# A new order, new buffers and new engines for every task of an RWKV and token-mixer kernel

## The chip, the cores and the metric

The kernel runs on one core of a Trainium2 chip. Its time is the device time of one execution in microseconds; the median of three runs of the kernel before is 160.68 us (159.12 to 160.82).

The engines are named as the profile names them: PE is TensorE's matmul stream and PEld its weight loads, DVE is VectorE, ACT is ScalarE, POOL is GpSimd, SP is SyncE, which here only issues DMAs. DMAs are issued from SP (loads of k, r and v, transposes, stores), from POOL (loads that also change the type: v of the first batch and all weights) and from ACT (small ones).

## The reference, cut to what matters

The inputs are r, k, v of 4 batches x 8 heads x 768 steps x 48 elements, and a decay w and a bonus u for each head and element. All are float32.

```python
for t in range(S):
    cur = einsum('bhd,bhe->bhde', u * k[t], v[t])
    y[t] = einsum('bhd,bhde->bhe', r[t], state + cur)
    state = w * state + einsum('bhd,bhe->bhde', k[t], v[t])
x = y as (4, 768, 384)
h = max(x.transpose @ w_tok1, 0) @ w_tok2        # 768 -> 256 -> 768, over the steps
u = x + h.transpose
out = u + max(u @ w_ch1, 0) @ w_ch2              # 384 -> 1536 -> 384
```

## The kernel before, in words

A batch is cut into six chunks of 128 steps. For a chunk, r and k are scaled by powers of the decay (tiles `kr`, one product on DVE or POOL for each), turned on PE or by a DMA, and multiplied with each other on PE to a 128 x 128 table of scores for each head (`at_ps`). DVE masks it (`AT`), PE multiplies it with v and adds what the state carries over (`y_ps`), and k and v are multiplied into the state (`kv_ps`). The term of u is a sum over r, u and k (`adg`), multiplied with v (`yd`, `ydb`). The result, `x_b`, goes to the mixer of the batch: two matmuls over the steps (`h_ps` from `wtok`, `hT_ps` or `hx_ps`), twelve blocks of "up" products for each half of the batch (`z_ps` from `wch`), each with a ReLU on ACT or DVE (`zr`), and the "down" products (`h_ps` from `zr`), with a sum on DVE or ACT and a store.

The first batch is done in pairs of chunks (`pair_unit`): three pairs of 256 steps, each with one load of k, one of r and one of v into the three parts of a tile `zr` (`room`, `homes`). Here the first pair's tile is `zr_121`, the second's `zr_104`, the third's `zr_163`; after the change they are `zr_104`, `zr_103` and `zr_105`. `load_v` issues the loads of v from POOL. In the second batch r is loaded in pairs too (`win`). The attention of a batch is interleaved with the mixer of the batch before it.

Every piece of work is a task with a number. `Plan.run` emits the tasks in the order of the table `ORDER`, and the engines keep that order. `BUFS` says which buffer each tile takes, and `ENGINES` which of two engines does each task that either may do. So the queues hold no surprise: what an engine does next is what stands next in its order, and it waits there until its inputs have come. `mul_k`, `mul_r` and `scaled` are the products into `kr`; `turned` and `turn_r` are the transposes on PE (`tk_ps`, `tr_ps`); `load_weights` issues the seven loads of weights, `w0` (w_tok1) to `w6` (last part of w_ch2).

`keep_warm` makes `NWARM` = 20 products of a tile of zeros (`warm`, 128 x 512) into a `kv_ps` bank. They are the zero products; nothing reads what they give.

All instructions of the kernel's body have the line 274 in the profile (276 after the change), so that they are told apart by their tiles.

The loop that emits the tasks, and the load of v:

```python
for n in self.order:
    emit, deps = self.tasks[n]
    assert done.issuperset(deps), n
    self.now = n
    emit()
    done.add(n)
...
t = homes[b, c][:, 2].bitcast(bf16)[:, 0:H // 2].rearrange("p h (z j d) -> p (h z) j d", z=2, j=2)
what = v[b, :, ds(c * T, 2 * T), :].rearrange("h (p j) d -> p h (j d)", j=2)
asked[b, c, 2] = pool.dma_start(t.rearrange("p h j d -> p h (j d)"), what)
```

Of the kernel before, what the change touches and what calls it, by code (L numbers as in the profile page):

```python
# [78 lines left out]
    0, 0, 0, 0,  # L79
    ],  # L80
    'adg': [
    0, 1, 2, 3, 4, 1, 0, 2, 3, 4, 1, 0, 2, 1, 3, 4, 0, 1,
    ],
    'adg2': [
    0, 1, 0,
# [1143 lines left out]
```

## Time and profile before

| | |
|---|---|
| median of the runs | 160.68 us (159.12 to 160.82) |
| span of the profiled execution | 157.6 us |
| time of that execution beyond its span | not shown by the page |
| PE busy | 152.7 us, 97% |
| DVE busy | 114.5 us, 73% |
| POOL busy | 78.0 us, 49% |
| ACT busy | 68.3 us, 43% |
| moved by DMA | 26.60 MB, mean 169 GB/s |

Times within the execution count from the start of its span. The chain of waits is followed back from the last instruction to what released it, and so on; it is shown in order of time. In a timeline, a bracket behind a row gives the idle time of the engine ahead of it and what ended it. A row may hold several instructions of one kind (x8); its length is then that of all. Instructions on PE overlap by their pipeline, so that the distance from one start to the next is what a piece costs.

### The profile page before, as it was taken

To read this page: it belongs to the slowest core of one execution; us is meant where nothing else is said; L and a number is where in the kernel's file an instruction comes from. 1 tells how busy PE (TensorE), PEld (TensorE's weight loads), DVE (VectorE), ACT (ScalarE), POOL (GpSimd) and SP (SyncE) were. 2 spreads that over 40 slices of the span, in tenths; PEclk is the share of its full clock that TensorE was granted. 3 is DMA by queue.
4 is the path that set the end of the run, shared out by engine and by line. 5 is a ranking of instruction groups with operands and counts; after the bars stand their busy time and mean duration, and the time that the engine had idled before them with its cause. 6 is when DMAs were issued, how large, how long until landed. Compare 5 with 4: busy or idle time off the path is not lost.

```text
span 157.6 us, 3939 instructions
## 1 busy us (share of the span) xinstructions
PE 152.7 (97%) x1564; PEld 102.4 (65%) x1564; DVE 114.5 (73%) x237; ACT 68.3 (43%) x154; POOL 78.0 (49%) x103
## 2 busy tenths in 40 slices
PE   6999999999999999999999999999999999999992
PEld 1375866777776676677767666677667666666661
DVE  5479894698697976889899978948998392544332
ACT  3876765749666363132851141179324102550100
POOL 7798689000996848945784445966814000000000
DMA  4999999999999999999999999999891066010423
GB/s 121 266 246 188 165 195 215 191 242 157 185 198 222 198 186 194 224 226 224 161 187 211 177 217 199 175 222 218 100 251 31 24 154 175 0 50 4 150 75 125
DMA packets 88005, 26.60 MB, mean 169 GB/s; under 512 B 82738, under 2 KB 87092, under 8 KB 87988
## 3 DMA queue, kind: packets, MB, share of 16 engines
q1 hardware_dynamic: 82512, 22.52, 73.8%
q0 software_dynamic: 5280, 3.74, 15.7%
q8 instruction: 12, 0.20, 0.5%
q10 hardware_dynamic: 196, 0.11, 0.2%
q14 instruction: 5, 0.04, 0.1%
HBM read 20.46 MB, written 4.72 MB: 160 GB/s over the span
## 4 chain that ended last, share of the span: by engine, by line
PE 95%; DVE 1%; ACT 1%; issue 1%; DVEq 0%; ACTq 0%
PE h_ps L274 36%; PE z_ps L274 30%; PE kv_ps L274 7%; PE y_ps L274 6%; PE at_ps L274 4%; PE hT_ps L274 4%; PE tr_ps L274 2%; PE hx_ps L274 2%; PE tk_ps L274 1%; PE w_ps L274 1%; PE trk L274 1%; PE ad_ps L274 1%; PE u_ps L274 1%; DVE pr L274 0%; ACT rkb L274 0%
## 5 line engine op out<-in xcount | busy, mean ns | idle before, releaser
L274 PE MATMUL h_ps<-wch,zr 128*128 128x384 bf16 (+1 forms) x300 | 52.7, 320 | 0.0
L274 PE MATMUL z_ps<-uT,wch 128*128 128x384 bf16 x288 | 50.5, 326 | 0.0
L274 ACT ACTIVATE zr<-z_ps 128x384 bf16<-128x384 f32 x63 | 28.5, 495 | 40.3 <-PE z_ps L274 40.2
L274 PEld LDWEIGHTS <-wch 128*128 128x128 bf16 x288 | 31.5, 114 | 12.5
L274 PEld LDWEIGHTS <-zr 128*128 128x128 bf16 x300 | 27.8, 98 | 16.1
L274 DVE TENSOR_SCALAR zr<-z_ps 128x384 bf16<-128x384 f32 x33 | 17.5, 553 | 9.8 <-PE z_ps L274 8.4
L274 DVE TENSOR_TENSOR AT<-at_ps,mask 128x512 bf16<-128x512 f32 x36 | 23.1, 684 | 1.4 <-PE at_ps L274 1.3
L274 POOL TENSOR_TENSOR kr<-kt,wnat 128x384 bf16<-128x384 f32 x13 | 13.0, 1004 | 9.9 <-DMA kt<-in_k_dram 4.3
L274 DVE TENSOR_TENSOR osb<-u_sb,h_ps 128x384 f32<-128x384 bf16 (+1 forms) x19 | 10.1, 531 | 9.6 <-PE h_ps L274 7.7
L274 POOL TENSOR_TENSOR yd<-vb,adg 128x384 f32<-128x384 bf16 x15 | 12.7, 849 | 7.3 <-ACT vb L274 5.8
L274 PEld LDWEIGHTS <-kr 128*128 128x128 bf16 (+1 forms) x196 | 12.4, 101 | 4.6 <-issue 1.8
L274 ACT CAST S<-kv_ps 48x192 bf16<-48x192 f32 (+1 forms) x26 | 8.8, 338 | 10.1 <-PE kv_ps L274 8.3
L274 POOL TENSOR_TENSOR ku<-kt,u_bc 128x384 f32<-128x384 f32 x10 | 9.9, 1001 | 4.4 <-DVE rku L274 2.8
L274 POOL TENSOR_TENSOR rku<-ku,rt 128x384 f32<-128x384 f32 x10 | 10.2, 1021 | 2.6 <-DVE ku L274 2.1
L274 PEld LDWEIGHTS <-wtok 128*128 128x128 bf16 x84 | 8.0, 98 | 5.1
L274 DVE TENSOR_TENSOR x_b<-y_ps,yd 128x384 bf16<-128x384 f32 x18 | 9.7, 553 | 2.2 <-PE y_ps L274 2.1
L274 DVE TENSOR_TENSOR u_sb<-x_b,hT_ps 128x384 bf16<-128x384 bf16 x18 | 8.9, 550 | 3.3 <-PE hT_ps L274 3.2
L274 POOL TENSOR_TENSOR kr<-rt,wp 128x384 bf16<-128x384 f32 x9 | 9.1, 1010 | 2.3 <-ACT wp L274 2.3
L274 ACT CAST vb<-vt 128x384 bf16<-128x384 f32 x14 | 7.1, 516 | 5.9 <-DMA vt<-in_v_dram 5.9
L274 PE MATMUL kv_ps<-warm 128*128 128x512 bf16 x20 | 8.0, 505 | 1.5 <-DVE warm L274 1.5
L274 PE MATMUL h_ps<-x_b,wtok 128*128 128x384 bf16 x48 | 8.6, 326 | 0.0
L274 DVE TENSOR_REDUCE adg<-rku 128x8 f32<-128x384 f32 x12 | 6.6, 546 | 1.7 <-POOL rku L274 1.7
(108 smaller groups left out, 189.3 us busy)
## 6 DMA issues: line engine op xcount, KB each, us to landing
out_dram<-osb SPq DMA_DIRECT2D x23, 192.0 KB, 2.3
kt<-in_k_dram SPq DMA_DIRECT2D x18, 192.0 KB, 5.6
vt<-in_v_dram SPq DMA_DIRECT2D x18, 192.0 KB, 3.9
rt<-in_r_dram SPq DMA_DIRECT2D x12, 192.0 KB, 3.8
wch<-in_moe_w_ch_dram POOLq DMA_DIRECT2D x4, 384.0 KB, 7.4
zr<-in_k_dram SPq DMA_DIRECT2D x3, 384.0 KB, 4.7
zr<-in_r_dram SPq DMA_DIRECT2D x3, 384.0 KB, 6.0
win<-in_r_dram SPq DMA_DIRECT2D x3, 384.0 KB
```

Of the source, the lines that this page charges most:

```text
L274: return lambda *args, **kw: tc.keep_in_program_order(f(*args, **kw))
```

## The change: what it does

All of `ORDER`, `BUFS` and `ENGINES` are new tables. The tasks and their number are the same, and so is the code that makes them. A line of each:

```diff
 ORDER = [
-    9, 57, 26, 3, 46, 0, 886, 884, 880, 1, 17, 8, 4, 6, 27, 24, 56, 59, 18, 19, 20, 10, 60, 2, 62, 878, 887,
...
+    3, 57, 56, 58, 60, 9, 49, 0, 45, 59, 8, 26, 881, 2, 10, 22, 62, 1, 880, 23, 42, 877, 63, 27, 4, 7,
...
     'kp': [
-    0, 1, 2, 3, 4, 5, 1, 3, 0, 5, 2, 1, 4, 3, 2, 0, 1, 5, 3, 4, 0, 2, 5, 0, 3, 1, 4,
+    0, 1, 2, 3, 4, 5, 1, 3, 0, 5, 1, 2, 4, 0, 3, 5, 2, 4, 0, 1, 3, 5, 2, 0, 4, 3, 1,
...
 ENGINES = [
-    0, 0, 0, 0, 1, 1, 0, 0, 1, 0, 1, 1, 0, 1, 0, 0, 0, 0, 1, 0, 1, 1, 0, 1, 0, 0, 0, 1, 0, 0, 0, 1, 0, 0, 0,
...
+    0, 0, 0, 0, 1, 0, 0, 1, 1, 1, 1, 1, 0, 0, 0, 1, 0, 0, 0, 0, 1, 1, 0, 0, 1, 0, 0, 0, 0, 0, 0, 0, 0,
```

Where the instructions then stand shows what moves. The first place is the start of POOL's order. Before, from its nineteenth row:

```order
L274 TENSOR_TENSOR kr0_67<-zr_121,u_sb_166 128x8x48
L274 MEMSET mask_80 128x128
L274 AFFINE_SELECT mask_80<-mask_80 128x128
L274 DMA zr_121<-in_v_dram 128x8x96
L274 DMA zr_104<-in_v_dram 128x8x96
L274 DMA zr_163<-in_v_dram 128x8x96
L274 TENSOR_TENSOR kr3_70<-zr_104,wpair_86 128x8x48
L274 TENSOR_TENSOR kr4_71<-zr_163,u_sb_166 128x8x48
L274 TENSOR_TENSOR wGm2_91<-bm_90,wG2_88 128x384
L274 TENSOR_TENSOR kr4_71<-zr_163,u_sb_114 128x8x48
L274 DMA wtok1_97<-in_moe_w_tok1_dram 128x6x256
L274 DMA wtok2_98<-in_moe_w_tok2_dram 128x1536
```

After, from its eleventh row:

```order
L276 MEMSET kr4_71 128x16x16
L276 DMA zr_104<-in_v_dram 128x8x96
L276 DMA zr_103<-in_v_dram 128x8x96
L276 DMA zr_105<-in_v_dram 128x8x96
L276 IOTA iota_i_76 128x2
L276 IOTA iota_i_76 128x3 x2
L276 IOTA iota_i_76 128x2
masks.py:199 AFFINE_SELECT ident_f_78<-ident_f_78 128x128
L276 DMA wtok1_97<-in_moe_w_tok1_dram 128x6x256
```

The three loads of v stand ahead of the last index tables and of every product, and w_tok1 follows them closely.

The second place is where POOL goes on, with the products of the third pair (`kr4` from its k, `kr5` from its r). After:

```order
L276 TENSOR_TENSOR kr3_70<-zr_103,wpair_86 128x8x48
L276 DMA wtok2_98<-in_moe_w_tok2_dram 128x1536
L276 TENSOR_TENSOR wGm2_91<-bm_90,wG2_88 128x384
L276 TENSOR_TENSOR kr4_71<-zr_105,u_sb_186 128x8x48
L276 TENSOR_TENSOR kr4_71<-zr_105,u_sb_189 128x8x48
L276 TENSOR_TENSOR kr5_72<-zr_105,wpair_86 128x8x48 x2
L276 TENSOR_TENSOR ydb_402<-zr_104,adg2_318 128x384
L276 DMA wch1_0_99<-in_moe_w_ch1_dram 128x3x512
```

Before, the rows above end with the two products into `kr4`; those into `kr5` were on DVE. Now POOL does all four, one behind another.

The third place is DVE in the middle of the first batch. Before:

```order
L274 TENSOR_TENSOR kr5_72<-zr_163,wpair_86 128x8x48
L274 TENSOR_TENSOR AT0_381<-at_ps_313,u_sb_123 128x512
L274 TENSOR_TENSOR kv_ps_349<-kv_ps_349,wGm2_91 128x384
L274 TENSOR_TENSOR pr2_480<-tr_ps_419,ka_417 128x1024
L274 TENSOR_TENSOR ydb_491<-zr_104,adg2_466 128x384
L274 TENSOR_TENSOR AT0_499<-at_ps_386,u_sb_123 128x512
```

After:

```order
L276 TENSOR_TENSOR ydb_400<-zr_104,adg2_318 128x384
L276 TENSOR_TENSOR kv_ps_327<-kv_ps_327,wGm2_91 128x384
L276 TENSOR_TENSOR pr2_453<-tr_ps_405,ka_375 128x1024
L276 TENSOR_TENSOR kr1_68<-win_145,wpair_86 128x8x48 x2
L276 TENSOR_TENSOR AT1_506<-at_ps_477,u_sb_148 128x512
L276 TENSOR_TENSOR AT0_520<-at_ps_476,u_sb_148 128x512
```

The two products of the second batch's first r (`kr1` from `win`), which stood on POOL, are on DVE now, ahead of masks of the second and third pair.

On PE the 20 zero products stand in stretches of 3, 3, 3, 1, 2, 1, 1, 1 and 5 before and of 3, 9, 2, 1, 1 and 4 after; between the first two stands the product that spreads w over the partitions (`w_ps`). On SP the order of the first seven loads is the same but for the first two, k and r of the first pair, which change places. Further on, loads, transposes and stores change places by a few rows.

More of the change, by code (lines that the diff above doesn't have):

```diff
@@ L66 @@
     'AT0': [
-    0, 1, 2, 0, 1, 0, 2, 0, 1, 0, 2, 1, 0, 2, 1, 2, 0, 2, 1, 0, 2, 1, 0, 1,
+    0, 1, 2, 0, 1, 0, 2, 0, 1, 0, 2, 1, 0, 1, 2, 0, 1, 2, 0, 1, 2, 0, 1, 2,
     ],
     'AT1': [
-    0, 1, 2, 0, 1, 0, 2, 0, 1, 2, 0, 1, 2, 0, 1, 0, 2, 0, 1, 2, 0, 2, 1, 0,
+    0, 1, 2, 0, 2, 0, 1, 0, 2, 1, 0, 2, 1, 2, 0, 1, 2, 0, 1, 2, 0, 1, 2, 0,
     ],
@@ L81 @@
     'adg': [
-    0, 1, 2, 3, 4, 1, 0, 2, 3, 4, 1, 0, 2, 1, 3, 4, 0, 1,
+    0, 1, 2, 3, 4, 0, 1, 3, 2, 4, 0, 3, 1, 4, 2, 0, 3, 1,
     ],
@@ L97 @@
     'kt': [
-    0, 1, 2, 3, 4, 5, 0, 1, 2, 3, 4, 0, 5, 1, 3, 2, 4, 0,
+    0, 1, 2, 3, 4, 5, 0, 1, 2, 3, 5, 4, 1, 2, 0, 3, 5, 4,
     ],
@@ L106 @@
     'm': [
[8 rows of a table removed]
[8 rows of a table added]
     ],
     'osb': [
-    0, 1, 2, 0, 1, 0, 1, 1, 1, 1, 2, 0, 0, 2, 1, 2, 0, 2, 0, 2, 0, 1, 2, 0, 1,
+    0, 1, 2, 1, 0, 2, 0, 1, 2, 0, 2, 1, 0, 2, 0, 1, 2, 2, 1, 2, 2, 1, 0, 2, 1,
     ],
     'pr': [
-    0, 1, 1, 0, 1, 0,
+    0, 1, 0, 1, 0, 1,
     ],
@@ L125 @@
     'rk': [
-    0, 1, 2, 3, 1, 0, 3, 2, 0, 1, 3, 2,
+    0, 1, 2, 3, 0, 1, 3, 2, 1, 0, 2, 3,
     ],
@@ L135 @@
     'rku': [
-    0, 1, 0, 0, 1, 0, 1, 0, 1, 0, 1, 0,
+    0, 1, 0, 1, 0, 1, 0, 1, 0, 0, 1, 1,
     ],
     'rt': [
-    0, 1, 2, 3, 4, 0, 2, 1, 3, 4, 0, 3,
+    0, 1, 2, 3, 4, 0, 1, 2, 3, 4, 1, 2,
     ],
@@ L145 @@
     'u_sb': [
-    0, 1, 2, 2, 0, 1, 2, 0, 1,
+    0, 1, 2, 1, 2, 0, 1, 2, 0,
     ],
     'vb': [
-    0, 1, 2, 3, 4, 0, 1, 2, 3, 0, 4, 2, 1, 4, 3, 2, 0, 4,
+    0, 1, 2, 3, 4, 0, 1, 2, 3, 4, 0, 2, 1, 3, 4, 2, 0, 1,
     ],
     'vt': [
-    0, 1, 2, 3, 4, 5, 0, 1, 2, 3, 4, 5, 0, 1, 2, 4, 3, 5,
+    0, 1, 2, 3, 4, 5, 0, 1, 2, 3, 4, 5, 0, 1, 3, 2, 4, 0,
     ],
@@ L157 @@
     'yd': [
-    0, 1, 2, 0, 1, 0, 2, 1, 0, 1, 2, 1, 0, 2, 1, 0, 2, 1,
+    0, 1, 2, 1, 0, 2, 1, 2, 0, 2, 1, 0, 2, 1, 0, 2, 1, 1,
     ],
```

116 rows, old and new, of tables (BUFS, ENGINES, ORDER) are left out of this document.

## The prediction

> **What bounds the kernel now.** I read the page first, then busy time by stretches, the chain that ended last, TensorE's own timeline of the first 26 us, and the DMA traffic in short stretches. The page gives the span, each engine's busy share, and the chain's split:
>
> ```profile
> span 157.6 us, 3939 instructions
> PE 152.7 (97%) x1564; PEld 102.4 (65%) x1564; DVE 114.5 (73%) x237; ACT 68.3 (43%) x154; POOL 78.0 (49%) x103
> PE 95%; DVE 1%; ACT 1%; issue 1%; DVEq 0%; ACTq 0%
> ```
>
> The same by stretches (stretch, its length, then busy us with instruction counts of PE, PEld, DVE, ACT and POOL, clock, DMA share, GB/s):
>
> ```profile
> 1.47:9.93 8.46, 8.46 (x31) 3.96 (x32) 5.40 (x22) 5.65 (x10) 7.13 (x19) 1.00 1.12 243
> 9.93:20.70 10.77, 10.52 (x214) 7.21 (x213) 9.21 (x19) 8.32 (x16) 8.32 (x11) 1.00 1.48 185
> ...
> 40.00:100.00 60.00, 60.00 (x613) 40.71 (x611) 50.77 (x99) 24.20 (x59) 41.69 (x46) 1.00 1.09 201
> 100.00:147.00 47.00, 47.00 (x384) 31.70 (x382) 30.70 (x60) 16.86 (x40) 13.12 (x15) 1.00 0.56 116
> ```
>
> From 40 to 147 us TensorE has no idle time. The change leaves its 1564 matmuls as they are, so no order gains there; it can only lose. What can be gained lies ahead of 26 us, and the chain (start, length, what) shows what that is:
>
> ```profile
> 6.42 1.39 PE kv_ps L274 x3
> ...
> 9.09 0.84 PE tr_ps L274 x8
> 9.93 0.43 PE kv_ps L274 x2
> 10.36 0.45 PE tk_ps L274 x8
> ...
> 21.24 0.35 PE at_ps L274 x16
> ```
>
> A zero product (kv_ps here) takes 0.46 us before 9.93 and 0.215 after it, eight transposes 0.84 and then 0.45: TensorE runs at half rate for its first 8.5 us, though the clock column reads 1.00 throughout. Half of that, 4.2 us, is one loss; the other is idle time, in the timeline rows that carry a bracket:
>
> ```profile
> 14.31 1.25 PE L274 MATMUL kv_ps<-warm 128*128 128x512 bf16 x5
> 15.62 0.50 PE L274 MATMUL kv_ps<-zr,kr 64*128 64x96 bf16 x8
> ...
> 17.58 0.62 PE L274 MATMUL tr_ps<-ident,kr 128*128 128x128 bf16 x8
> 18.03 0.33 PE L274 MATMUL y_ps<-S,rkb 128*128 128x96 bf16 x4
> ...
> 20.75 0.50 PE L274 MATMUL kv_ps<-zr,kr 64*128 64x96 bf16 x8 [0.20 <-ACT S L274]
> ...
> 22.80 0.79 PE L274 MATMUL tr_ps<-ident,kr 128*128 128x128 bf16 x8
> 23.52 0.51 PE L274 MATMUL kv_ps<-zr,kr 64*128 64x96 bf16 x8
> 23.97 0.83 PE L274 MATMUL h_ps<-x_b,wtok 128*128 128x384 bf16 x4
> ...
> 25.72 0.50 PE L274 MATMUL y_ps<-zr,AT 64*128 64x48 bf16 x26 [0.24 <-issue]
> ```
>
> That is 0.20 + 0.24 = 0.44 us. The page gives a span and no time of its own for this execution; the median of the runs, 160.68, lies 3.1 us above the span, and I add 3.1 to every span below.
>
> **The change part by part.** *v of the first batch* is three loads that GpSimd issues (one for each pair of chunks). What they share the DMA engines with decides the case, so first the traffic. The first row is q1 (the queues of SP) in 0 to 5.65 us, the second q1 alone in 4 to 10; then q0 (GpSimd's queue) and q1 in 10.6 to 18.6 (v), 18.7 to 21.6 (w_tok1) and 21.6 to 24.4 (w_tok2). Columns: packets, MB, share.
>
> ```profile
> q1 hardware_dynamic: 2455, 0.93, 71.1%
> ...
> q1 hardware_dynamic: 4176, 1.58, 126.5%
> ...
> q0 software_dynamic: 3040, 0.58, 83.0%
> q1 hardware_dynamic: 3064, 0.84, 68.9%
> ...
> q0 software_dynamic: 766, 0.39, 97.8%
> q1 hardware_dynamic: 735, 0.14, 39.7%
> ...
> q0 software_dynamic: 301, 0.49, 93.7%
> q1 hardware_dynamic: 297, 0.06, 17.8%
> ```
>
> Alone, q1 moves 4176/6 = 696 packets a us. With q0 active the two get packet for packet the same: 380 a us each beside v, 253 beside w_tok1 (larger packets), 106 beside w_tok2. Each load of a pair is 1024 packets (128 partitions x 8 heads). When they are issued and land (start and length on the engine; then, of one load each, the time from issue to landing: the third pair's r, the first v):
>
> ```profile
> 5.92 1.44 SPq L274 DMA_DIRECT2D zr<-in_r_dram  x1
> ...
> 2.65 0.31 POOL L274 MEMSET u_sb<- 128x256 bf16 x1
> ...
> 7.39 2.85 POOL L274 DMA_DIRECT2D zr<-in_v_dram  x3
> ...
> zr<-in_r_dram SPq DMA_DIRECT2D x1, 384.0 KB, 6.3
> ...
> zr<-in_v_dram POOLq DMA_DIRECT2D x1, 192.0 KB, 6.7
> ```
>
> Before, v is issued behind six loads of k and r, which are 6144 packets. The third r lands at 5.92 + 6.3 = 12.2. Its last packet: 2455 at 5.65, 5900 at 10.6, the other 244 at 380 a us, so 11.25; a landing comes 0.95 behind the last packet. The first v lands at 14.1; less 0.95 and 1024/380 = 2.7 its first packet is at 10.45, 3.1 after its issue.
>
> Now v is issued behind the rows that stood before 2.65, so its packets begin at 5.75, when q1 has sent 2525. The 3072 packets of v take 8.1 us; q1 sends as many, and stands at 5600 at 13.85. GpSimd has issued w_tok1 right behind v, so the 544 packets that the third r still lacks go at 253 a us: last at 16.0, landing at 16.95 and not 12.2. The second batch's first r (win), the next load on q1, needs 7168: at 16.75, when w_tok1 is through, q1 has 6335; w_tok2 lets 297 through until 19.55; the other 536 alone take 0.8. It lands at 21.25. In return v lands 4.7 earlier. That it was late costs little before: the products that read v start at 15.62, behind five zero products from 14.31 on, when v has been there since 14.1.
>
> By the Trainium skill, "DMA: Bandwidth & Descriptors", section "Anatomy of one DMA", a DMA from GpSimd takes about 2.0 us plus its bytes over 436 GB/s; for 196,608 B that gives 2.45 us, and three of them would hold the others up by some 1.4 us, the third r landing at 13.6, which is the first rival below. The row of 6.7 us does not agree with it.
>
> *The products of the third pair's r* stood on DVE and now stand on GpSimd, behind its two products of k:
>
> ```profile
> 16.19 0.55 DVE L274 TENSOR_TENSOR kr<-zr,wpair 128x384 bf16<-128x384 f32 x1
> ...
> 21.19 1.95 POOL L274 TENSOR_TENSOR kr<-win,wpair 128x384 bf16<-128x384 f32 x2
> ```
>
> Two on GpSimd take 1.95 us: 16.95 + 1.95 = 18.9. TensorE transposes them (17.58 before) at 18.95. Work in front of it is the same but for one score product (at_ps, 0.35 us) that now comes behind. Behind it come five pieces that filled 18.03 to 20.55 before: 18.95 + 0.45 + 2.52 = 21.92. Then stands the transposition of the next r load, whose two products moved from GpSimd to DVE (1.0 us): ready at 21.25 + 1.02 = 22.3, a wait of 0.4. From there to the first hidden product TensorE has what filled 20.75 to 23.97, 3.22 us, less 0.27 (those transposes took 0.72 and not 0.45, waiting for GpSimd), plus the 0.35: 3.3, so 25.6 for 23.97. The stall of 0.24 at 25.72 would be covered: masks done meanwhile. Sum: 25.6 - 23.97 - 0.24 = +1.4 us. Bounds: -1.4 (nothing waits, and the half rate ends sooner) and +3.8, both worked out below.
>
> *The zero products* are 20 as before. The runs are 3, 3, 3, 1, 2, 1, 1, 1, 5 before and 3, 9, 2, 1, 1, 4 now. Full rate came after an unbroken stretch from 6.42 to 9.93; now one begins at about 4.5. I take 0 for it: TensorE waits for the third r at 17.5 to 18.9 whatever it saved ahead of that.
>
> *Everything later.* Nothing can be gained there. Three bounds on losses. DVE has 13 more ReLUs (49 for 36) and fewer stand on ACT; its fullest stretch before was 80 to 100 us, 17.74 of 20, with TensorE still at 20.00:
>
> ```profile
> 80.00:100.00 20.00, 20.00 (x208) 12.94 (x207) 17.74 (x35) 5.07 (x14) 11.51 (x13) 1.00 1.13 201
> ```
>
> 13 x 0.55 us (the DVE row above has the same size) spread over the span leave DVE below that share on average; 0 to 0.5, I take 0. The first part of w_ch2 is issued behind one product on GpSimd:
>
> ```profile
> 40.84 1.15 POOL L274 DMA_DIRECT2D wch<-in_moe_w_ch_dram  x2
> ...
> wch<-in_moe_w_ch_dram POOLq DMA_DIRECT2D x1, 384.0 KB, 5.8
> ...
> 47.68 0.65 PE h_ps L274 x4
> ```
>
> It lands at 46.64, 1.0 ahead of its first reader, and that reader moves up by about 1.2 us of TensorE's work, counted in the order, against the product that gates the issue: 0 to 0.3, I take 0. The third batch's and fourth batch's loads keep their places on SP within a few rows, 0. The tail (one DVE sum, one store) is unchanged.
>
> **The rivals.** *No wait comes.* If the k and r loads keep their pace (the skill's fit would say so), the third r's products end at 12.2 + 1.95 = 14.2 at the earliest and, behind the two of k, by about 15.5; TensorE comes to them no sooner and only loses its 0.44 of idle time: 157.6 - 0.4 + 3.1 = 160.3. Against it: 3040 packets to 3064, even over 8 us. Chance 0.22.
>
> *The half rate ends sooner and nothing waits.* From 4.5 the 3.5 us that were enough before end at 8.0 and not 9.93; half of 1.9 is saved: 156.2, or 159.3. The Trainium skill, "TensorE: Matmul & The Clock Gate", Part 1, has the rate double after a busy window of about 3.4 us that runs free of the kernel's start; by that, the end lies anywhere from 7.9 to 11.3, and the trace's 3.5 us agree. Against it: it needs the first rival too. Chance 0.10, half of it under 159.07.
>
> *w_tok2 catches the third r (slower).* Its 6144th packet is sent 0.75 us before w_tok1 ends. If v's packets begin half a us sooner, or k and r get some 6% less, its last packets go at 106 a us and it lands by up to 2.8 us later, at 19.75: transposes at 21.75, first hidden product at 21.75 + 0.45 + 2.52 + 3.3 = 28.0, +3.8 with the 0.24: 164.5. It decides from the landing at 17.7 on. Chance 0.20.
>
> That the change does not do what it says is not one: v stands at the twelfth row of GpSimd's order.
>
> **How the numbers follow.** The forecast, chance 0.48: 157.6 + 1.4 = 159.0 of span, 162.1 us, its own range 161.2 to 163.2. One per cent, about what a measurement tells from no change, is 159.07 to 162.29. Slower: 0.20 of the last rival and 0.20 of the forecast's upper part, 0.40. Faster: 0.06. The rest, 0.54, is within 1%. The range of 159.6 to 164.5 leaves out the lower half of the second rival and the last rival's excess.
>
> **What would show it.** In the changed kernel: v's packets from about 5.8 us and the first v landed by 9.5; q1 and q0 equal from there to 14; the third r landing at 16 to 18; TensorE's idle before the third pair's r transposes, released by GpSimd's kr, with a start of 18.5 to 19.5; the first hidden product at 25 to 26; no idle from 30 to 150. If the third r lands at 12 to 14, the sharing was read wrongly; if TensorE idles after 40, the part on later stages was.

## The result, and the profile after

The changed kernel is slower: the ratio to the kernel before is 1.0488 [1.042, 1.0555]. Its four runs took 167.62, 168.26, 171.06 and 171.53 us, those of the kernel before on the same chip 160.31 in the median; the two longest, whose mean granted clock was 0.97, are left out of the ratio, and with them the median is 169.66. The four lie 3.9 us apart, as far as most of the experiments below lie from each other, so that these are read from the rows of their profiles as well as from their ratios. The prediction was 162.1 us with a range of 159.6 to 164.5.

The profiled execution is the one of 167.62 us. Its span is 8.3 us longer than before (165.9 for 157.6) where 1.4 were forecast. The page:

```profile
span 165.9 us, 3946 instructions
...
PE 155.3 (94%) x1564; PEld 102.9 (62%) x1564; DVE 130.6 (79%) x257; ACT 61.2 (37%) x140; POOL 79.2 (48%) x98
...
PEclk9987999999999999999999999999999999999999
...
PE 33%; DMA 3%; DVE 0%; issue 0%
```

DVE is busy 16.1 us more than before and ACT 7.1 less, and the chain that ended last no longer runs through TensorE to the start: it comes to an end at a DMA, of which more below. The clock line has an 8 and a 7 near the start. By stretches of the changed kernel (columns as in the prediction):

```profile
8.23:11.47 3.24, 0.97 (x11) 0.74 (x10) 1.56 (x5) 0.00 (x0) 0.94 (x2) 1.00 1.44 196
11.47:14.88 3.41, 3.41 (x25) 2.79 (x24) 2.77 (x7) 2.48 (x5) 3.39 (x4) 0.50 1.45 193
...
40.00:60.00 20.00, 19.41 (x214) 13.68 (x213) 19.36 (x39) 12.00 (x28) 8.43 (x10) 1.00 1.06 192
60.00:100.00 40.00, 39.38 (x375) 26.20 (x374) 36.59 (x67) 14.40 (x36) 27.94 (x28) 1.00 0.97 192
100.00:163.00 63.00, 60.89 (x492) 40.43 (x489) 43.86 (x87) 11.62 (x28) 17.11 (x19) 1.00 0.48 109
```

Three things are new. TensorE is busy 0.97 of 3.24 us from 8.23 on; right behind that its clock is 0.50 for 3.41 us; and it has idle time after 40 us, with DVE at 19.36 of 20 in the first 20 of them. TensorE's rows up to the first hidden product (h_ps from x_b):

```profile
4.26 3.97 PE L276 MATMUL kv_ps<-warm 128*128 128x512 bf16 x9
10.29 0.35 PE L276 MATMUL ud_ps<-ident_f,wp 8*128 8x8 f32 x2 [2.06 <-DVE wp L276]
...
11.18 0.40 PE L276 MATMUL tr_ps<-ident,kr 128*128 128x128 bf16 x4 [0.21 <-DVE kr L276]
...
18.89 0.91 PE L276 MATMUL u_ps<-wp,ones 1*128 1x384 f32 x2
...
20.46 0.62 PE L276 MATMUL tr_ps<-ident,kr 128*128 128x128 bf16 x8
...
24.35 0.40 PE L276 MATMUL tr_ps<-ident,kr 128*128 128x128 bf16 x4 [0.70 <-DVE kr L276]
...
27.55 0.82 PE L276 MATMUL h_ps<-x_b,wtok 128*128 128x384 bf16 x4
```

The largest wait, 2.06 us, is one that the prediction does not name: the small product `ud_ps` waits for a product of DVE on the rows of u. Who was late there, with the issues on ACT and the wait on DVE:

```profile
4.37 0.32 ACTq L276 DMA_DIRECT2D wp<-in_u_dram  x1
...
4.90 0.24 ACTq L276 DMA_DIRECT2D wp<-in_u_dram  x1
...
9.91 0.28 DVE L276 TENSOR_TENSOR wp<-wp 8x128 f32<-8x128 f32 x1 [2.05 <-DMA wp<-in_u_dram]
```

Before, ACT issued both of u's small loads at once:

```profile
1.90 0.59 ACTq L274 DMA_DIRECT2D wp<-in_u_dram  x2
```

In the new order they stand behind ACT's first logarithm; the first is issued at 4.37, into queues that v, k and r fill, and DVE has what it needs at 9.9. The wait at the third pair's r (20.46) is not there; the one at win's transposes (24.35) is, with 0.70.

Where the 8.3 us lie, by TensorE's first product of each kind. The columns are the first hidden product of batch one, its first "up" product, the first hidden products of batches two and three, and the end of the span:

| | hidden 1 | up 1 | hidden 2 | hidden 3 | end |
|---|---|---|---|---|---|
| before | 23.97 | 32.20 | 57.71 | 89.76 | 157.6 |
| after | 27.55 | 35.21 | 62.49 | 95.78 | 165.9 |
| lost in the stretch | 3.58 | -0.57 | 1.77 | 1.24 | 2.28 |

Of the first 3.58 us, 2.77 are idle time (2.06 + 0.21 + 0.70, less the 0.20 of before) and 0.94 are half rate: 6.94 us of the start and 3.41 at 11.47 are run at half rate, 10.35 for 8.46 before, and half of the difference is lost. TensorE starts 0.18 earlier. The other 4.7 us are lost later, where the prediction had 0. Of the last 2.28, 1.82 are one wait at 107.86, for the transposed input of an "up" product (uT). The waits of PE, with total, count and longest:

```profile
PE ud_ps L276 <- DVE wp L276: 2.1, 1, 2.1
PE z_ps L276 <- DMA uT<-u_sb: 1.8, 1, 1.8
...
PE tr_ps L276 <- DVE kr L276: 1.1, 3, 0.7
```

### The profile page after: what moved, and what is told of

It reads as the page before. It is cut to its first block, busy times and chain, and to the rows that moved or that the text cites. A ratio compares the mean times of both kernels' runs of the same rounds, so it can differ in the third digit from the quotient of the medians.

```text
span 165.9 us, 3946 instructions
## 1 busy us (share of the span) xinstructions
PE 155.3 (94%) x1564; PEld 102.9 (62%) x1564; DVE 130.6 (79%) x257; ACT 61.2 (37%) x140; POOL 79.2 (48%) x98
## 3 DMA queue, kind: packets, MB, share of 16 engines
HBM read 20.46 MB, written 4.72 MB: 152 GB/s over the span
## 5 line engine op out<-in xcount | busy, mean ns | idle before, releaser
L276 PE MATMUL z_ps<-uT,wch 128*128 128x384 bf16 x288 | 51.9, 326 | 2.1 <-DMA uT<-u_sb 1.8
L276 ACT ACTIVATE zr<-z_ps 128x384 bf16<-128x384 f32 x50 | 23.0, 493 | 45.6 <-PE z_ps L276 44.9
L276 DVE TENSOR_SCALAR zr<-z_ps 128x384 bf16<-128x384 f32 x46 | 24.0, 550 | 8.5 <-PE z_ps L276 8.0
L276 POOL TENSOR_TENSOR yd<-vb,adg 128x384 f32<-128x384 bf16 x12 | 10.7, 891 | 21.2 <-ACT vb L276 10.0
L276 ACT CAST S<-kv_ps 48x192 bf16<-48x192 f32 (+1 forms) x29 | 9.9, 341 | 13.8 <-PE y_ps L276 5.6
L276 POOL TENSOR_TENSOR kr<-kt,wnat 128x384 bf16<-128x384 f32 x13 | 13.8, 1071 | 0.0
L276 POOL TENSOR_TENSOR ku<-kt,u_bc 128x384 f32<-128x384 f32 x11 | 11.8, 1084 | 2.9 <-DVE zr L276 2.9
L276 POOL TENSOR_TENSOR pr<-rka,rkb 128x512 bf16<-128x512 bf16 x3 | 3.5, 1166 | 12.2 <-DVE kv_ps L276 7.6
L276 DVE TENSOR_TENSOR AT<-at_ps,u_sb 128x512 bf16<-128x512 f32 x12 | 7.6, 680 | 1.2 <-PE at_ps L276 1.2
L276 POOL TENSOR_TENSOR rku<-ku,rt 128x384 f32<-128x384 f32 x6 | 6.2, 1030 | 3.2 <-DMA rt<-in_r_dram 3.1
```

The lines of the kernel that those rows point to most:

```text
L276: return lambda *args, **kw: tc.keep_in_program_order(f(*args, **kw))
```

## The experiments

All ratios are to runs of the kernel before on the same chip, whose medians were 159.4 to 159.7 us.

**The start.** The theory after the first look: the early loss is two supplies, u's row and the loads of k, r and win that v holds up, and the half rate is a consequence of waiting. *Only u's loads early*, on ACT:

```diff
 L276 DMA wp<-in_w_dram 8x2x48
+L276 DMA wp<-in_u_dram 8x2x48
+L276 DMA wp<-in_u_dram 1x384
 L276 ACT_TABLE_LOAD
 L276 ACTIVATE lnw<-w_ps 128x384
-L276 DMA wp<-in_u_dram 8x2x48
 L276 ACTIVATE u_sb<-lnw,iota 128x384
-L276 DMA wp<-in_u_dram 1x384
 L276 ACTIVATE u_sb<-lnw,iota 128x384
```

> The changed kernel with one edit: ACT issues the two loads of u right behind those of w, as the kernel before did. Theory (two stalls side by side): the wait of 2.06 us for u's small product and the return of the half rate (11.4 to 14.7 us) go, and TensorE comes to the transposes of the third pair's r at 8.23 + (20.46 - 10.29) - 0.21 - 1.65 = 16.5 us and not 20.46. But that r lands at 17.9 and GpSimd has its two products at 19.86, and the second batch's first r is ready at 24.35 as now; so the wait only moves there, the first hidden product stays at 27.0 to 27.6 and the span at 165 to 166 us (27.55 and 165.9 now). Rival (the load of u alone is the loss of the first stage): first hidden product at 27.55 - 2.27 - 1.65 = 23.6, span 162.0.

Measured: 1.0659 [1.0581, 1.0737], no gain: its four runs, 169.26 to 170.77 us, lie within those of the changed kernel. The first hidden product comes at 29.54, later than theory and rival had it. The wait for u is gone, and TensorE comes to the wait that the prediction had named, for the products of the third pair's r on GpSimd (its timeline and GpSimd's):

```profile
19.35 0.61 PE L276 MATMUL tr_ps<-ident,kr 128*128 128x128 bf16 x4 [1.20 <-POOL kr L276]
20.30 0.61 PE L276 MATMUL tr_ps<-ident,kr 128*128 128x128 bf16 x4 [0.34 <-POOL kr L276]
...
18.13 2.12 POOL L276 TENSOR_TENSOR kr<-zr,wpair 128x384 bf16<-128x384 f32 x2 [2.16 <-DMA zr<-in_r_dram]
```

So the mechanism of the forecast exists and was covered by an earlier wait. Around that wait the clock falls to 0.50, and for three times as long as in the changed kernel:

```profile
18.94:29.18 10.24, 9.33 (x174) 7.02 (x175) 6.76 (x10) 3.53 (x8) 8.21 (x12) 0.50 1.15 206
```

Half of the busy 9.33 us is 4.7 us lost, for 1.7 in the changed kernel.

*Only v late*, on GpSimd:

```diff
 L276 MEMSET kr_71 128x16x16
-L276 DMA zr<-in_v_dram 128x8x96 x3
 L276 IOTA iota_i 128x2
...
-L276 DMA wtok_97<-in_moe_w_tok_dram 128x6x256
 L276 MEMSET u_sb 128x256
 L276 AFFINE_SELECT u_sb<-u_sb 64x256 x2
+L276 DMA zr<-in_v_dram 128x8x96 x3
...
 L276 TENSOR_TENSOR kr_71<-zr,u_sb 128x8x48 x2
+L276 DMA wtok_97<-in_moe_w_tok_dram 128x6x256
```

> The changed kernel with one edit: GpSimd issues the three loads of v behind the second of its two early masks (about 8 us and not 2.65) and w_tok1 behind its two products of the third pair's k. Theory (two stalls side by side): k and r of the first batch keep their pace, the third pair's r lands at 12 to 13.5 and the second batch's first r by 16; u's rows still land late, since the loads of SP alone fill the queues; TensorE still waits about 2 us for u's product, its wait of 0.70 at 24.35 goes: first hidden product 26.85, span 165.2. Rival (it is v's packets that hold u's rows up): u lands by 8.5, no wait, no return of the half rate, first hidden product at 23 to 24, span 161 to 162. Second rival (v late is itself a new wait): y products of the first pair wait for v at 16 to 18 us, span over 165.9.

Measured: 1.047 [1.037, 1.0569], the profiled span 164.2, the first hidden product at 26.48. v was issued at 4.5 us and not at the 8 of the expectation, since the rows ahead of it are short. The wait for u falls to 1.18 us, so that the early v makes a part of it and not all. The one of 0.70 ahead of win's transposes stays, against the theory, and half rate comes from 11.61 to 15.02 as it does in the changed kernel from 11.47; the ratio tells no gain from the noise. *Both edits together*:

> The changed kernel with both edits, u's loads early and v's late. Theory (two stalls side by side, each hiding the other): all of 2.27 + 0.70 + 1.65 = 4.6 us comes back; first hidden product 22.9 us, span 161.3; what is left against the kernel before, 3.7, is of the later stages. Rival (the later stages take back what the first saves, since DVE sets their pace): first hidden product the same, but span over 163.5.

Measured: 1.0529 [1.0442, 1.0617], again no gain clear of noise, and the first hidden product at 26.62 where the theory had 22.9. Neither of the two waits is left ahead of 20 us. But TensorE now waits 1.13 and 0.70 us for win, and half rate follows that wait, as it follows the later one for uT (the stretches around each, in order of time):

```profile
20.05:23.46 3.41, 1.57 (x46) 1.19 (x46) 2.88 (x5) 1.44 (x5) 2.88 (x3) 1.00 1.32 199
23.46:26.87 3.41, 3.41 (x60) 2.52 (x58) 3.41 (x6) 1.05 (x3) 2.62 (x3) 0.50 1.14 203
105.50:108.79 3.29, 0.70 (x6) 0.50 (x6) 2.56 (x6) 0.00 (x0) 3.29 (x4) 1.00 1.21 154
108.79:112.20 3.41, 3.41 (x19) 1.79 (x18) 0.63 (x2) 1.98 (x5) 2.17 (x3) 0.50 1.05 213
```

*The change's place of v alone, in the kernel before*, on GpSimd:

```diff
 L274 AFFINE_SELECT u_sb<-u_sb 64x256 x2
+L274 DMA zr<-in_v_dram 128x8x96 x3
 L274 MEMSET u_sb 128x256
...
+L274 DMA wtok_97<-in_moe_w_tok_dram 128x6x256
 L274 MEMSET kr_71 128x16x16
 L274 TENSOR_TENSOR kr_67<-zr,u_sb 128x8x48
...
-L274 DMA zr<-in_v_dram 128x8x96 x3
 L274 TENSOR_TENSOR kr_70<-zr,wpair 128x8x48
...
-L274 DMA wtok_97<-in_moe_w_tok_dram 128x6x256
 L274 DMA wtok_98<-in_moe_w_tok_dram 128x1536
```

> The kernel before with one part of the change: GpSimd issues the loads of v behind its first mask (about 2.6 us) and w_tok1 behind its index tables; all else as before, so DVE still makes the products of the third pair's r. Theory (the sharing of the queues costs what the prediction priced): third pair's r lands at 17 to 18 us, its transposes start at 18.5 to 19.1 (17.58 before), first hidden product 24.9 to 25.5 (23.97 before), span 158.5 to 159.2. Rival (no wait comes, the zero products and other work cover it): span 157.3 to 157.9.

Measured: 1.0231 [1.0147, 1.0314], 3.7 us of span where the theory had 0.9 to 1.6, and by another way. The third pair's r is not waited for. GpSimd spends 2.85 us issuing v and 0.89 issuing w_tok1 ahead of its first product, which starts at 8.63 and not 5.76, and TensorE waits for that one:

```profile
9.87 1.03 PE L274 MATMUL tk_ps<-ident,kr 128*128 128x128 bf16 x8 [1.72 <-POOL kr L274]
```

It does so in the half rate of the start, which lasts to about 13.9 us for 9.93 and has 10.45 us of work in it for 8.46, so that some 1.0 us more is lost to it. Of the 3.2 us by which the first hidden product is later (27.19), the two make 2.7. The price of an early v was thus, in this order, first of all GpSimd's own time, not the share of the DMA engines. In the changed kernel that price doesn't show: there GpSimd's first product stands idle for 2.30 us until an r has landed.

**Behind 30 us.** DVE is nearly full there in the changed kernel, and engines were chosen anew for 128 of 293 tasks. Theory: those choices cost the late 4 us; rival: order and choices belong together, or the wait only moves. *The change with the choices of before*, and *before with the choices of the change*, both only for tasks behind the first "up" product (99 and 102 entries of the table); of the first, part of DVE's order, of the second another:

```diff
-L276 CAST vb<-vt 128x384
-L276 COPY rka<-trk 128x512
-L276 TENSOR_TENSOR x_b_96<-y_ps,yd 128x384
-L276 TENSOR_SCALAR zr<-z_ps 128x384
-L276 TENSOR_TENSOR pr<-trk,rkb 128x512
+L276 TENSOR_TENSOR pr<-trk,rkb 128x512
+L276 COPY rka<-trk 128x512
+L276 TENSOR_TENSOR x_b_96<-y_ps,yd 128x384
...
+L274 TENSOR_SCALAR zr<-z_ps 128x384
+L274 COPY adg<-ad_ps 128x8
 L274 COPY rka<-trk 128x512
```

> The changed kernel with the engine choices of the kernel before for every task that stands behind the first up product (order and buffers stay those of the change): 33 ReLUs go from DVE to ACT and 20 the other way, 9 casts of v from DVE to ACT, 12 products from DVE to GpSimd and 7 back. Theory (DVE, full from 40 to 60 us, sets TensorE's pace there and costs 1.9 us between the first up product and the second batch's hidden products, and 1.2 us more up to the third's): from the first up product (z_ps) to the second batch's x12 hidden products 25.3 to 25.8 us (27.28 now, 25.35 before), from these to the third batch's 32.0 to 32.5 (33.29 now), span about 163. Rival (the new order and buffers cost it, whatever engine does the work): 27.0 to 27.5 and 33.1 to 33.5, span 165 to 166.

> The kernel before with the engine choices of the change behind the first up product, order and buffers as before. Theory (the engine choices alone make DVE late): from the first up product to the second batch's hidden products 26.5 to 27.5 us (25.35 before), span 159.1 to 160.7. Rival (they cost only together with the new order): 25.3 to 25.6, span 157.3 to 158.0.

Measured: 1.0567 [1.0512, 1.0622] and 1.0675 [1.0595, 1.0756]. The first gains nothing: from the first "up" to the second batch's hidden product it takes 27.55 us (27.28 after, 25.51 before), though DVE is busy for only 21.66 of the 25 us from 35 to 60 (24.28 after). The second loses far more than either theory had; eight waits of 0.44 to 2.05 us for DVE appear, the longest of them

```profile
91.44 0.34 PE L274 MATMUL h_ps<-wch,zr 128*128 128x384 bf16 x1 [2.05 <-DVE zr L274]
```

So an engine choice has no price of its own here: it is good or bad with the order that it was made for, and these two runs can't divide the late loss between the tables.

*The wait for uT*: its transpose and a store ahead of three loads on SP.

```diff
 L276 DMA_TRANSPOSE rk<-kr_72 128x8x128
+L276 DMA out_dram<-osb 128x384
+L276 DMA_TRANSPOSE uT<-u_sb 128x9x128
 L276 DMA kt<-in_k_dram 128x8x48
 L276 DMA rt<-in_r_dram 128x8x48
 L276 DMA vt<-in_v_dram 128x8x48
-L276 DMA out_dram<-osb 128x384
-L276 DMA_TRANSPOSE uT<-u_sb 128x9x128
```

> The changed kernel with one edit on SP: the transposition of the third batch's first half of u_sb stands ahead of the three loads (k, r, v) that stood close in front of it. Theory (its landing took 5.2 us and not 3.2 because three loads and a store were in the queue ahead of it): it lands 3.2 to 3.5 us behind its issue, the wait of 1.82 us at 107.86 is 0 to 0.5, span 164.0 to 164.5 with the same clock at the start. Rival (it waits for its last sum on DVE, not for the queue, or the loads then come too late for the fourth batch): wait still 1.5 or a new one of that size, span 165.5 or more.

Measured: 1.0733 [1.0652, 1.0814]. The wait for uT is gone, and in its place stands one for v of the fourth batch. Its load is not one of the three, but stands behind them on SP: it is issued at 110.09 (106.45 in the changed kernel) and lands at 113.34.

```profile
113.81 0.33 PE L276 MATMUL kv_ps<-vb,kr 128*128 128x96 bf16 x4 [2.37 <-DVE vb L276]
```

The rival held: what is put ahead on SP holds up what stands behind. *u early and v in two parts* (against the first experiment's order, on GpSimd):

```diff
-L276 DMA zr<-in_v_dram 128x8x96 x3
+L276 DMA zr<-in_v_dram 128x8x96
...
-L276 DMA wtok_97<-in_moe_w_tok_dram 128x6x256
...
 L276 TENSOR_TENSOR kr_70<-zr,wpair 128x8x48
-L276 DMA wtok_98<-in_moe_w_tok_dram 128x1536
+L276 DMA zr<-in_v_dram 128x8x96 x2
...
 L276 TENSOR_TENSOR kr_71<-zr,u_sb 128x8x48 x2
+L276 DMA wtok_97<-in_moe_w_tok_dram 128x6x256
+L276 DMA wtok_98<-in_moe_w_tok_dram 128x1536
```

> The changed kernel with u's loads early, the first load of v where the change has it, the other two behind GpSimd's product of the second pair, and both w_tok loads behind its two products of the third pair's k. Theory (the idle times of the first 25 us are landings, and each idle time of a microsecond or more is followed by one or more stretches of 3.4 us at half rate): the third pair's r lands at 12.5 to 14.5 and the second batch's first r by 18, TensorE has no idle time of over 0.6 us between 8 and 30 us, no clock of 0.50 there, first hidden product at 22.9 to 24.0 us, span 161 to 162.5. Rival (v's second and third pair then land too late, 17 to 19 us): a wait at the third pair's or second pair's state products, first hidden product past 25, span over 163.

Measured: 1.0654 [1.0573, 1.0736]. The theory missed: no wait behind the first microseconds and ahead of 28 us is longer than 0.74, and yet TensorE runs at half rate from 18.12 to 28.36, behind 3.41 us of which 2.91 were busy. "Half rate follows a long wait" was therefore not the whole rule.

**Two halves.** *The change up to the first hidden product and the kernel before behind it*, and *the reverse*. Of the order table, the place where the first turns from the one to the other, and then that of the second:

```diff
-    181, 193, 207, 202, 197, 73, 194, 322, 180, 311,
+    181, 193, 38, 73, 197, 202, 180, 207, 212, 203,
...
-    200, 202, 180, 207, 212, 196, 193, 203, 194, 204,
+    200, 202, 180, 72, 76, 39, 41, 44, 196, 320,
```

> A splice: order and engines of the changed kernel up to the first hidden product, and from there the order and engines of the kernel before (buffers dealt out anew in that order). Theory (the loss is two separate ones, early and late): first hidden product at 27 to 28.5 us (27.55 in the changed kernel, 23.97 before), from it to the end 133.4 to 134.2 (133.6 before, 138.4 in the changed kernel), span 160.5 to 162.5. Rival (what the late part loses it loses because the early part is late, loads and sums being behind): span 164 or more.

> The opposite splice: the kernel before up to the first hidden product, and from there the order and engines of the change. Theory (two separate losses): first hidden product at 23.9 to 24.1, no clock of 0.50 ahead of it, from it to the end 137.5 to 139, span 161.5 to 163, with a wait of 1.3 to 2.6 us for a transposed uT between 98 and 106. Rival (the late loss follows from the early one): span 157.5 to 158.5.

Measured: 1.0356 [1.0287, 1.0426] and 1.0442 [1.0363, 1.0522]. The early half alone keeps the early loss, its first hidden product at 28.14, and then takes 134.6 us to the end where the kernel before takes 133.6 and the changed one 138.4: of the late 4.7 us all but 1.0 are not carried over from the start, but belong to the late half of the tables. The late half alone shows a late loss without the early one (23.51 to the first hidden product), but not its size: the seam, where one order turns into the other, makes a wait of its own of 2.63 us, and the wait for uT is 2.63 too. Its best run, with a mean clock of 1.0, had a span of 164.7. *The late half with stores put behind loads and transposes on SP*:

```diff
-L276 DMA out_dram<-osb 128x384 x2
+L276 DMA rt<-in_r_dram 128x8x48
+L276 DMA vt<-in_v_dram 128x8x48
+L276 DMA rt<-in_r_dram 128x8x48
 L276 DMA_TRANSPOSE rk<-kr_72 128x8x128
 L276 DMA_TRANSPOSE rk<-kr_68 128x8x128
+L276 DMA out_dram<-osb 128x384 x2
+L276 DMA_TRANSPOSE uT<-u_sb 128x9x128
...
```

> The splice with the late part of the change and one edit on SP: the first two stores, for whose sums SP stood still for 4.3 us in the changed kernel (58.8 to 63.3, no DMA moved a byte from 62 to 64), go behind the first three loads and two transpositions that stood after them. Theory (the time in which SP stands still is what later lacks: 4 us of loads at some 200 GB/s, so the transposed uT and v of the fourth batch come late at 100 to 114 us): no stretch without DMA traffic at 56 to 62, wait for uT at most 0.5, span 1.5 to 2.5 under that of the unedited splice. Rival (the loads moved up wait for their buffers, or the late waits come from elsewhere): wait for uT as in the unedited splice, span within 0.7 of it.

Measured: 1.0573 [1.0531, 1.0615] beside 1.0442 [1.0363, 1.0522] without this edit. The wait for uT is 1.19 us, and one of 1.49 for DVE at 76.08 and one of 0.49 for weights come instead: a loss and no gain, where the theory had a gain and the rival no change.

**Waits without half rate.** *Both edits of the start, and zero products in the waits that stay*: 5 ahead of win's transposes and 14 ahead of the third batch's first "up" product. They add work that nothing reads. The table, and what it is used for:

```diff
-FILL = {}
+FILL = {310: 5, 605: 14}
...
+    for i in range(FILL.get(plan.now, 0)):
+        pe.matmul(bank, warm[:, 0:128], warm[:, 0:bank.shape[-1]], start=fresh, stop=True, skip_group_check=True)
```

> The changed kernel with u's loads early and v's late (as run before: idle 1.13 + 0.70 us ahead of 22.3 us and 2.59 ahead of 108.1, each followed by 3.4 us at a clock of 0.50; span 167.7), and zero products put into these waits, into banks that are overwritten right behind them: 5 of 512 columns ahead of the transposes of the second batch's first r, 14 of 384 columns ahead of the third batch's first up product. More work, in time that was idle. Theory (it is TensorE's idleness that brings the half rate back, and each stretch costs 1.7 us): no clock of 0.50 after 20 us but at the very end, mean clock 0.995 or more, span 163.8 to 164.8. Rival (idle time and half rate have another common cause, or idle time alone counts): stretches of 0.50 as before, span 167 to 168.

Measured: 1.0406 [1.0358, 1.0455], span 164.5 as expected; the median is 166.43 us for 168.36 without the 19 products, on another chip. More work on TensorE makes the kernel faster by some 1.9 us, because the clock stays: the two stretches of 3.41 us at half rate are gone, half of which is 3.4 us, and the profiled spans differ by 3.2 (the stretch around the wait for uT; compare the last two rows of the stretches of "both" above):

```profile
100.00:115.00 15.00, 15.00 (x131) 10.29 (x130) 12.41 (x25) 3.12 (x8) 9.78 (x11) 1.00 1.14 222
```

*win's transposes behind the first batch's work again, and no zero products there* (DVE's side of it):

```diff
 L276 TENSOR_TENSOR pr_453<-tr_ps,ka 128x1024
+L276 TENSOR_TENSOR AT_504<-at_ps,u_sb 128x512
+L276 TENSOR_TENSOR AT_509<-at_ps,u_sb 128x512
+L276 TENSOR_TENSOR AT_550<-at_ps,u_sb 128x512
+L276 TENSOR_TENSOR kv_ps<-kv_ps,wGm_91 128x384
 L276 TENSOR_TENSOR kr_68<-win,wpair 128x8x48 x2
...
```

> The changed kernel with u's loads early, v's late and 14 zero products in the wait for the third batch's transposed u (run before with 5 more zero products ahead of the transposes of the second batch's first r: first hidden product 25.90, span 164.5), and one edit: those transposes go, on TensorE, from ahead of two score products of the first batch to behind its last state product, where the kernel before has them, and their two products on DVE go behind three masks; the 5 zero products are gone. Theory (that r, held up by v and w_tok, lands at 20.4 in any case; what costs is that the new order puts its transposes ahead of 2 us of work that was ready): no idle over 0.5 us between 18 and 26, first hidden product at 23.2 to 24.2, span 162.0 to 163.0. Rival (the work behind them waits for something else as late as that): first hidden product at 25.3 or later, span 164 to 165.

Measured: 1.0393 [1.0345, 1.0441]. The wait for win is gone as the theory said, but the first hidden product comes at 26.47 (25.90 without the edit), where the theory had 23.2 to 24.2. The gain is eaten in the profiled run by half rate, and ahead of that half rate TensorE is idle for 0.24 us of 3.41:

```profile
14.30:17.71 3.41, 3.17 (x55) 2.14 (x52) 3.41 (x6) 2.81 (x7) 3.08 (x4) 1.00 1.36 203
17.71:27.95 10.24, 10.24 (x181) 7.74 (x178) 7.96 (x13) 5.03 (x12) 7.59 (x10) 0.50 1.16 191
```

Its fastest run has a mean clock of 1.0 and a span of 163.7.

*The DVE, relieved*: to the kernel with zero products, four casts of the second batch's v and a copy from DVE to ACT, two products of yd from DVE to GpSimd.

```diff
-L276 CAST vb<-vt 128x384
...
-L276 COPY adg<-ad_ps 128x8
...
-L276 TENSOR_TENSOR yd<-vb,adg 128x384 x2
```

> The changed kernel with u's loads early, v's late and zero products in both waits (span 164.5; from the first up product to the second batch's hidden products 27.30 us, 25.35 in the kernel before), and one edit: of the second batch's attention four casts of v go from DVE to ACT, two products yd from DVE to GpSimd and one small copy to ACT, as the kernel before has them; about 4.2 us of DVE's work between 43 and 60 us. Theory (DVE, busy 95 to 100% there, sets the pace): that stretch takes 25.4 to 26.2 us, span 162.7 to 163.7. Rival (the order of the rows makes TensorE wait, whatever DVE's load; when all later engine choices were put back it did not gain either): 27.0 or more, span 164.2 to 164.8.

> Both edits of the two kernels beside it. If both theories hold and the gains add: first hidden product at 23.2 to 24.2, first up product to the second batch's hidden products 25.4 to 26.2 us, span 160.3 to 161.5; if only the first holds, 162 to 163; if what is won early is given back by loads that come no earlier, 163 or more.

Measured: 1.0429 [1.0387, 1.0471], and with the edit of win as well 1.0405 [1.0366, 1.0443]. Three times the stretch from 35 to 60 us: before, with zero products, and with DVE relieved:

```profile
35.00:60.00 25.00, 25.00 (x285) 17.82 (x284) 20.33 (x42) 15.81 (x39) 15.64 (x18) 1.00 1.05 190
```

```profile
35.00:60.00 25.00, 24.39 (x275) 17.38 (x274) 24.01 (x46) 14.47 (x33) 9.82 (x11) 1.00 1.05 198
```

```profile
35.00:60.00 25.00, 24.70 (x281) 17.67 (x280) 20.38 (x41) 16.73 (x39) 10.89 (x14) 1.00 1.07 199
```

DVE falls from 24.01 to 20.38 us, and the way from the first "up" to the second batch's hidden product from 27.30 to 26.24 (25.51 before). So 1.06 of the 1.77 us lost there come back when these seven tasks leave DVE (0.98 and 1.47 in the two later runs that have the edit as well). That DVE's load alone set the pace does not follow, since the run with the choices of before had a load nearly as small and gained nothing. The total does not show the gain: the median is 166.42 us beside 166.43 without the edit. The profiled execution has half rate from 18.44 to 25.27, but the other three, with a mean clock of 1.0, took 165.78 to 166.64, so that half rate alone does not hide it; what else hides it stays open. With win's edit the first hidden product comes at 24.87, and half rate from 17.52 to 20.93.

**Zero products, and one product of a single row.** What is left at the start is half rate with little or no waiting ahead of it. Two runs in the kernel before: *zero products in runs of 3, 9, 2, 1, 1 and 4*, and *`u_ps` moved*, the product that spreads u over the partitions, from among zero products to behind the third pair's k, where the change has it; ACT's copy of its result (`u_bc`) goes with it, and the buffers are dealt out anew for that order:

```diff
-L274 MATMUL u_ps<-wp,ones 128x384
 L274 LDWEIGHTS warm
 L274 MATMUL kv_ps<-warm 128x512
...
 L274 MATMUL tk_ps<-ident,kr_71 128x128
+L274 MATMUL u_ps<-wp,ones 128x384
```

> The kernel before with its 20 zero products placed in the runs of the change: 3, 9 (behind the product that spreads w), 2, 1, 1 and 4, these last ahead of the product that spreads u; nothing else moved. Theory of the prediction (the places of the zero products are worth 0): span 157.3 to 158.2, first hidden product at 23.7 to 24.5. Rival (they keep TensorE's activity up in stretches of thin products, those with 1, 48 or 64 rows or 8 columns; gathered early, a stretch from 14 to 18 us falls short and half rate returns for 3.4 us or more in some runs): a clock of 0.50 between 15 and 30 us in the profile, or a mean clock of 0.99 or less in some of the runs, span 159 to 161.

> The kernel before with one product moved on TensorE: the one that spreads u over the partitions (one row, 384 columns in float32, 0.84 us) goes from among the zero products to behind the transposes of the third pair's k, where the change has it. Theory (the stretch of 3.4 us with this product, sums of 8 columns and state products of 64 rows is too thin to hold the full rate): a clock of 0.50 for 3.4 us or more between 16 and 30 us in the profile or a mean clock of 0.99 or less in some of the runs, span 159 to 161 there. Rival (thin products count as work like any other): clock 0.997 or more in all runs, span 157.3 to 158.2.

Measured: 1.0039 [1.0002, 1.0076] for the zero products, with a mean clock of 1.0: 0.6 us (0.0 to 1.2), where the prediction had 0; the first hidden product comes at 24.88. For `u_ps` 1.0142 [1.0098, 1.0186], in all five runs with a mean clock of 0.968 to 0.979. One product of 0.84 us, moved, costs more than all zero products:

```profile
15.10:18.57 3.47, 3.00 (x52) 2.17 (x51) 2.01 (x6) 1.91 (x5) 2.84 (x4) 1.00 1.53 153
...
18.59:28.83 10.24, 10.24 (x167) 7.06 (x165) 6.91 (x12) 5.18 (x13) 7.00 (x8) 0.50 1.20 202
```

In the kernel before, the first of these stretches is

```profile
15.10:18.57 3.47, 3.41 (x85) 2.69 (x83) 3.03 (x8) 2.04 (x6) 2.44 (x4) 1.00 1.52 153
```

and the clock stays. With `u_ps` there it has 0.47 us of idle time and `u_ps` itself, a product of one row, where 33 instructions more stood before. The idle time comes with the move, too: TensorE waits for ACT's cast `S`, which now stands behind the copy of `u_ps`:

```profile
17.68 0.50 PE L274 MATMUL kv_ps<-zr,kr 64*128 64x96 bf16 x8 [0.47 <-ACT S L274]
...
16.61 0.48 ACT L274 COPY u_bc<-u_ps 128x384 f32<-128x384 f32 x1 [2.62 <-PE u_ps L274]
```

That it is the product of one row, and not the idle time, that brings half rate is thus not shown. *The reverse in the changed kernel* (that with win and DVE mended):

```diff
+L276 MATMUL u_ps<-wp,ones 128x384
 L276 LDWEIGHTS warm
 L276 MATMUL kv_ps<-warm 128x512
...
 L276 MATMUL tk_ps<-ident,kr_71 128x128
-L276 MATMUL u_ps<-wp,ones 128x384
```

> The changed kernel with all edits so far (u's loads early, v's late, the second batch's first transposes put back, seven of DVE's tasks put back, 14 zero products in the wait for uT; span 164.3 with a stretch of half rate from 17.5 to 20.9 us), and the product that spreads u moved up to ahead of its last four zero products. Theory (thin stretch): no clock of 0.50 between 12 and 30 us, mean clock 0.995 or more in all or all but one of the runs, first hidden product at 23.0 to 24.2, span 162.0 to 163.3. Rival (it is idle time and chance alone): a stretch of half rate there as before, clocks of 0.98 to 0.99 in half of the runs, span 164 to 165.

Measured: 1.0406 [1.0363, 1.0449]. Three of five runs keep a clock of 1.0, for one of four without this edit, but the time is the same, and the profiled run has half rate from 23.95 to 27.36 behind an idle time of 0.65. It settles nothing: with the change's order half rate comes at another place.

No kernel that was run beats the kernel before. The lowest ratio that an edit of the changed kernel reached, 1.0393 with win's, is 1.5 us under the 7.8 us that 1.0488 stands for; by the medians of all runs the edits take back 2.8 of 9.4 us.

## Why the prediction was wrong

**That TensorE bounds the kernel and can only lose after 40 us** was right, and "Everything later: 0" was the step that failed by most: 4.7 us. Two of its three bounds asked the right engine and took the wrong end. The 13 ReLUs on DVE were spread over the whole span; the page before and the page after show that DVE is busy for 16.1 us more, and for 24.28 of the 25 us from 35 to 60, where it had 20.33. The runs show that 1.0 to 1.5 us come back when seven tasks leave DVE, but not that its load alone is the cause. SP's loads "keep their places within a few rows, 0" hid a wait of 1.8 us for uT; the two runs that changed SP's order show that other waits come in its place, but not what would remove it. That the late half of the tables costs most of the 4.7 us is shown by the run that puts the kernel before behind the first hidden product; for the 1.24 us between the second and the third batch no run shows which part of them does.

**That v early makes the two queues share packet for packet** was right. In the changed kernel, from 5.8 to 10 and from 10 to 14 us:

```profile
q0 software_dynamic: 1579, 0.30, 83.3%
q1 hardware_dynamic: 1590, 0.60, 70.3%
...
q0 software_dynamic: 1347, 0.26, 73.0%
q1 hardware_dynamic: 1345, 0.51, 72.8%
```

It fits what the Trainium skill states ("DMA: Bandwidth & Descriptors", section "Queues, rings and completion order": an engine serves the queues in turn and takes a whole packet from each). A packet of that page holds several descriptors; whether the packets that the profile counts are those is not shown here. The third pair's r was forecast to land at 16.95 and win at 21.25; the engines that wait for them start at 17.9 and 22.35, 1 us later each:

```profile
17.90 1.96 POOL L276 TENSOR_TENSOR kr<-zr,wpair 128x384 bf16<-128x384 f32 x2 [1.10 <-DMA zr<-in_r_dram]
...
22.35 1.94 DVE L276 TENSOR_TENSOR kr<-win,wpair 128x384 bf16<-128x384 f32 x2 [0.23 <-DMA win<-in_r_dram]
```

The forecast had too little for the sharing with w_tok1: from 15 to 17 us SP's queue sends 449 packets, 225 a us where 253 were taken.

**The wait at the third pair's r, 18.9** does not appear, since TensorE is held up by 2.06 us before it and arrives at 20.46. The step that failed is one that is missing: the part by part counts GpSimd's, DVE's, SP's and TensorE's moves, and nothing of ACT's, where u's two loads stand. The run that put them back shows the forecast's wait (1.20 + 0.34 us). It is no faster for that: with u in time, the next wait and a longer half rate took the place of the first.

**The wait at win, 0.4**, was the right mechanism, and 0.70. Part of the difference is the price of DVE's two products: 1.02 us were taken, and here the two take 1.94, as the row above shows, with GpSimd busy beside them; whether that is the reason was not tried. The forecast's first hidden product, 25.6, came at 27.55.

**The clock** was priced once, at the start, and taken as full from there on. The return of half rate costs 1.7 us for each 3.41 us of it, and is in the profiled run after a wait of 2.06 us. It is not all of the loss: the run of 168.26 us has a mean clock of 1.0 and is no shorter.

**The rivals.** "No wait comes" and "half rate ends sooner" (9.93 before; here the nine zero products run at half rate to their end at 8.2, and what was saved was idled away) both fell by the wait for u. Of "w_tok2 catches the third r" the landing past 17.7 came, but not by w_tok2: up to 18.05 us no packet of 2 KB or more has been sent, w_tok2's are 3 KB each, and the products of that r start at 17.9. Nor did the wait that it names decide.

**Zero products, 0**, was about right (0.6 us in the kernel before). **The 3.1 us between span and time** were 1.7 in the changed kernel's profiled execution (167.62 - 165.9) and 1.7 to 2.0 in the experiments; with 1.7 the forecast would have been 160.7, further off.

## What to carry to other kernels

When a schedule is replaced, read the new order of every engine that issues loads, the smallest loads too: a load of 3 KB, issued 2.5 us later into full queues, made the longest wait of the start, and putting it back alone gained nothing, because the next wait stood close behind. A wait on TensorE can cost more than its length, since half rate can follow it, and products that nothing reads, put into the wait, can pay for themselves. A bound on an engine's load has to be made in the stretch where its work is, not over the span.

## What the runs showed of the hardware

After the start, half rate comes in stretches of 3.41 us or two or three times that, and the edges of one run lie on one grid: 26.87 and 112.20 in "both" are 25 x 3.413 apart, 15.29, 28.94 and 117.69 in the run on uT 4 and 26 x 3.413. The Trainium skill, "TensorE: Matmul & The Clock Gate", Part 1, names a free-running window of 3413 ns; the runs agree on the period. For the fall to half rate it names at least one idle window. Here it fell after windows that were 33% busy (1.14 of 3.41 us, from 8.06 in the changed kernel), 46% (1.57 of 3.41), and 93% (3.17 of 3.41); with 19 zero products in the waits it did not fall. What the hardware counts, and why a return to full rate takes one window in one run and three in another, stays open.

How long a landing takes differs by a factor from place to place: the three loads of v, 192 KB each, took 6.0, 8.2 and 10.4 us from issue in the changed kernel (6.7, 8.4 and 10.2 before), and the transposing DMA of uT issued at 102.64 took 5.2 us, where two later ones took 3.2. And GpSimd needs about 0.95 us to issue each of v's loads (2.85 for three), time in which it does no product.
